# Duplicated feature columns by load, inverse deviations column by column, and x transposes between the tiles of the output projection, in a one-core adaLN transformer block

## The chip, the cores and the metric

The kernel runs on one core of a Trainium2 chip. The metric is the device time of one execution in microseconds (us). The core's engines are TensorE (PE in the rows; PEld its weight loads), VectorE (DVE), ScalarE (ACT), GpSimd (POOL) and SyncE (SP), which here issues nearly all DMAs.

## The reference

```python
mod = silu(c) @ w_mod                    # six vectors of 448: sa, ca, ga, sb, cb, gb
h = layernorm(x) * (1 + ca) + sa         # x: 2048 x 448, float32
q, k, v = split(h @ wqkv)                # 16 heads of 28
p = softmax(mask(q @ k.T * 28**-0.5))    # a key lies at most 255 positions back
x = x + ga * ((p @ v) @ wo)
h = layernorm(x) * (1 + cb) + sb
x = x + gb * (mish(h @ w1 + b1) @ w2)    # w1: 448 x 1792, w2: 1792 x 448
```

## The kernel before

The 2048 rows are worked through in four groups (g) of 512 rows, each four tiles of 128. Every product is done with split operands: a matrix is held as a high part (`hh`, `oh`, `wq3`, `Ph`) and the rest (`hl`, `ol`, `wql`, `Pl`), and a tile of a projection is eleven matmuls. The 448 features lie in four chunks of 128; the last chunk holds its 64 features twice, so that its high and low part share a matmul. That is why a normed row has 512 columns, the last 64 a copy of columns 384 to 447.

For a group, `gen_ln` (L226) takes the statistics of four row tiles on VectorE (`ln_stats`, L218), forms the inverse deviations `rs` on POOL (an add of epsilon, L234, and a power of -0.5, L235, each over four columns), norms the tiles on VectorE (L241), and copies the 64 columns on POOL (`dup`, L223). For the first norm that is done in place in `xin` (`gen_ln1`, L272), for group 0 of the second norm in `x1` (`gen_ln2`, L853); groups 1 to 3 of the second norm go by another way through DRAM (`gen_x1_ln2`, L1105). `gen_hT` (L287) then transposes the group's x on TensorE, one chunk of four 128x128 transposes per bank, two banks of the tag "mm" in turn; per chunk ScalarE makes `hh` (`hT_hi`, L256), and VectorE the scaled value in the bank (`hT_y`, L253) and `hl` (`hT_lo`, L259), after which the bank is free.

The attention is a hand-written loop over 192 units u, three per head and 48 per group. In a unit TensorE makes a block of scores (`B`, sB), the scores for a running maximum of a later head (`A`, sA; VectorE reduces them into mx, the line of junk), and the product with V of an earlier unit (`PV`); ScalarE makes P and Ph, and POOL one subtraction Pl = P - Ph (`SP`, L731). Between them the loop places other work, the fillers: `fill_main(g)` (L937) yields, for group g, the last three q/k tiles of g, then `gen_oT(g - 1)` (L614: transposes of the attention's output and their split), `gen_wo(g - 1)` (L637: the output projection by four tiles, whose sum with x, `xr`, and statistics `stw` VectorE takes), `gen_hT(g + 1)` and the first q/k and V tiles of g + 1. Each filler step names its cost in us, and each unit adds `RATE[g]` (L979) to a credit; steps are placed while the credit lasts. A second generator, `fill_side(g)` (L958), places small work once per unit. `pipe` (L29) delays the steps that follow a filler's matmuls by one step each.

The engines take their instructions in the order in which this program issues them, and SP its DMAs too. The tiles oT of the attention's output have the same names and buffers ("hh", "hl" of the pool `mid`) as the split x, so one waits for the readers of the other.

After the 192 units comes the second layer: 56 blocks n (14 per group) of a first product z, Mish on ScalarE and a second product acc.

## Time and profile before

| | |
|---|---|
| median of 3 runs | 708.94 us (708.24 to 710.24) |
| profiled execution | 708.93 us, of which the span 707.1 us |
| TensorE busy | 687.4 us |
| VectorE / ScalarE / POOL busy | 384.0 / 391.4 / 326.0 us |
| granted clock of TensorE | 1.00 of full speed |

The profile gives the busy time of each engine, in the whole span and in any window of it, the instructions in order of time with the idle time before each and what ended it, and groups of instructions by line, operation and shape with their mean duration. The attention of groups 0 to 3 takes the time to about 410 us, the second layer the rest.

### The profile page before, as it was taken

Reading aid. Unit: us, or ns where it says so; the run is one execution under the profiler, and the core shown is the slowest. Engines: PE = TensorE matmul, PEld = TensorE weight load, DVE = VectorE, ACT = ScalarE, POOL = GpSimd, SP = SyncE. Lnnn points to the kernel's source line nnn. Section 1 sums busy time; section 2 is a strip of 40 time slices with the busy share of each in tenths; the row PEclk is TensorE's granted clock in tenths of the full one; section 3 lists DMA queues with packets and bytes.
Section 4 is the critical chain, followed back from the end, with each engine's and each line's share of the span. In section 5 each row is a group of like instructions: output and inputs, shape, how many; then the busy total and the mean of one; then the engine's idle time right before and its main releaser. Section 6 shows DMA issues by size and latency. Waiting matters only on the chain.

```text
span 707.1 us, 12019 instructions
## 1 busy us (share of the span) xinstructions
PE 687.4 (97%) x4001; PEld 589.0 (83%) x4001; DVE 384.0 (54%) x1030; ACT 391.4 (55%) x740; POOL 326.0 (46%) x355
## 2 busy tenths in 40 slices
PE   8899999999999999999999999999999999999997
PEld 8777888888898788898887788887888888888886
DVE  5688667688664888555767765452314222422112
ACT  3638778767766867767877974344223322332221
POOL 6626779586766677666778957313010000000000
PEclk9999999999999999999999999999999999999999
DMA  7865664454672462762774155810340035001001
GB/s 211 256 224 182 216 198 160 136 163 151 191 214 71 152 194 91 189 208 78 230 217 141 54 195 159 238 25 1 104 110 10 1 105 116 4 1 52 1 1 52
DMA packets 75177, 90.16 MB, mean 127 GB/s; under 512 B 31534, under 2 KB 51740, under 8 KB 75116
## 3 DMA queue, kind: packets, MB, share of 16 engines
q1 hardware_dynamic: 74652, 89.39, 42.1%
q8 instruction: 32, 0.52, 0.3%
q14 instruction: 29, 0.24, 0.1%
q10 hardware_dynamic: 464, 0.00, 0.0%
HBM read 56.60 MB, written 32.51 MB: 126 GB/s over the span
## 4 chain that ended last, share of the span: by engine, by line
PE 77%; DVE 9%; ACT 4%; issue 3%; POOL 1%; DMA 0%; DVEq 0%; ACTq 0%; POOLq 0%
PE z L913 19%; PE pv L741 9%; PE qk L315 8%; PE acc L1098 6%; PE acc L1096 6%; PE acc L1097 6%; PE sA L679 5%; PE sB L709 4%; PE wo L315 4%; PE qk_v L315 4%; PE sB L720 3%; DVE junk L681 3%; PE et L755 2%; ACT P L723 1%; ACT Ph L724 1%
## 5 line engine op out<-in xcount | busy, mean ns | idle before, releaser
L731 POOL TENSOR_TENSOR Pl<-P,Ph 128x512 fp32r<-128x512 f32 (+2 forms) x192 | 234.3, 1228 | 83.2 <-ACT Ph L724 44.7
L681 DVE CUSTOM_DVE_ANT_0 junk<-sA,mask 128x384 f32<-128x384 f32 (+2 forms) x256 | 135.2, 528 | 96.5 <-PE sA L679 88.3
L723 ACT ACTIVATE P<-sB 128x512 f32<-128x512 f32 (+2 forms) x192 | 109.8, 572 | 63.3 <-PE sB L720 58.3
L921 DVE TENSOR_TENSOR al<-t,ah 128x512 fp32r<-128x512 f32 x56 | 39.2, 700 | 181.8 <-ACT ah L920 181.8
L919 ACT ACTIVATE t<-z,b1c 128x512 f32<-128x512 f32 x56 | 38.3, 684 | 138.6 <-PE z L913 138.6
L724 ACT ACTIVATE Ph<-sB 128x512 fp32r<-128x512 f32 (+2 forms) x192 | 109.2, 569 | 0.0
L679 PE MATMUL sA<-k,q 84*128 84x384 f32 (+2 forms) x256 | 100.9, 396 | 2.3 <-DVE mx L681 1.5
L913 PE MATMUL z<-hlf,w 128*128 128x512 f32 x224 | 88.5, 395 | 0.0
L913 PE MATMUL z<-hhf,w 128*128 128x512 f32 x224 | 88.5, 395 | 0.0
L1096 PE MATMUL acc<-w2h,ah 128*128 128x448 f32 x224 | 82.2, 367 | 1.2 <-ACT ah L920 1.2
L1098 PE MATMUL acc<-w2h,al 128*128 128x448 f32 x224 | 82.0, 366 | 0.0
L1097 PE MATMUL acc<-w2l,ah 128*128 128x448 f32 x224 | 81.5, 364 | 0.0
L741 PE MATMUL pv<-Pl,v 128*60 128x256 f32 (+2 forms) x352 | 74.0, 284 | 3.8 <-POOL Pl L731 2.8
L741 PE MATMUL pv<-Ph,v 128*60 128x256 f32 (+2 forms) x352 | 76.6, 291 | 0.6 <-ACT o L747 0.5
L709 PE MATMUL sB<-q,k 86*128 86x256 f32 (+1 forms) x352 | 74.0, 284 | 0.2
L913 PE MATMUL z<-hhf,w1l 128*128 128x512 f32 x168 | 66.2, 394 | 0.0
L709 PEld LDWEIGHTS sB<-q,k 86*128 86x128 f32 x352 | 61.5, 189 | 1.8 <-issue 0.6
L720 PE MATMUL sB<-fdmask,identr 128*128 128x128 bf16 (+1 forms) x320 | 60.1, 253 | 0.0
L741 PEld LDWEIGHTS pv<-Ph,v 128*60 128x60 f32 x352 | 45.5, 133 | 14.6 <-ACT o L747 2.4
L679 PEld LDWEIGHTS sA<-k,q 84*128 84x128 f32 x256 | 48.9, 192 | 8.7 <-DVE mx L681 6.0
L741 PEld LDWEIGHTS pv<-Pl,v 128*60 128x60 f32 x352 | 45.0, 131 | 13.2 <-POOL Pl L731 5.4
L913 PEld LDWEIGHTS z<-hlf,w 128*128 128x128 f32 x224 | 42.1, 188 | 10.1
(159 smaller groups left out, 1249.8 us busy)
## 6 DMA issues: line engine op xcount, KB each, us to landing
scr<-st SPq DMA_DIRECT2D x24, 512.0 KB
k<-scr SPq DMA_DIRECT2D x48, 252.0 KB
q<-scr SPq DMA_DIRECT2D x64, 168.0 KB
scr<-st SPq DMA_DIRECT2D x32, 256.0 KB
x<-x1d SPq DMA_DIRECT2D x10, 448.0 KB
xin<-in_A_x_dram SPq DMA_DIRECT2D x8, 448.0 KB
xr<-in_A_x_dram SPq DMA_DIRECT2D x16, 224.0 KB
x1d<-xr SPq DMA_DIRECT2D x16, 224.0 KB
```

The costliest lines, as they stand in the source:

```text
L315: PE.matmul(p, b, a, start=(n == 0), stop=(n == 10))
L679: PE.matmul(p[:, c0:384], q[0:84, t * 128:(t + 1) * 128], k[0:84, t * 128 + c0:t * 128 + 384], start=True, stop=True)
L681: DVE.tensor_tensor_reduce(out=junk[:, c0:384], in0=p[:, c0:384], in1=mask[:, c0:384], scale=1.0, scalar=-3.0e38, op0=ALU.add, op1=ALU.max ...
L709: PE.matmul(p[:, c:c + 128 * (t1 - t0)], k[:, jj * 128:(jj + 1) * 128], q[:, t0 * 128:t1 * 128], start=(n == 0), stop=False, skip_group_ch ...
L723: ACT.activation(P[:, c0:], p[:, c0:], AF.Exp, scale=SCALE)
L724: ACT.activation(Ph[u][:, c0:], p[:, c0:], AF.Exp, scale=SCALE)
L731: eng.tensor_tensor(Pl[u][:, a:b], Pt[u][:, a:b], Ph[u][:, a:b].bitcast(F32), op=ALU.subtract)
L741: PE.matmul(pv[0:60, t0 * 128:t1 * 128], V[j % NV][:, h, :], P[u][:, c:c + 128 * (t1 - t0)], start=(P is Ph and b == 0 and n == 0), stop=F ...
L913: PE.matmul(zb[n], ps[m][1], ps[m][0], start=(m == 0), stop=(m == 10))
L1096: PE.matmul(p, ah[n][:, ts], w2h[f], start=(f == 0), stop=False)
L1097: PE.matmul(p, ah[n][:, ts], w2l[f], start=False, stop=False)
L1098: PE.matmul(p, al[n][:, ts], w2h[f], start=False, stop=(f == NF - 1))
```

## The change

The loads of x for groups 1 to 3 (`x_half`), and of x1 for group 0 of the second norm (`x1_load`), get a second DMA that brings features 384 to 447 into columns 448 to 511; the norm there works in place on all 512 columns (`wide`), without `dup`. The inverse deviations are made column by column: VectorE adds epsilon to one column (`rs_add`), POOL raises it to -0.5 (`rs_pow`), one step later in `gen_ln`. For group 0 of the second norm they are made ahead, at the end of group 1's side work (`gen_rs2`). `gen_wo` takes a generator `beside` and places one step of it after each tile: for groups 1 and 2 that is `gen_hT(g + 1)`, one chunk after each tile of the output projection. The split output of the attention gets tiles of its own (tags "hho", "hlo" in the pool `att`), `ol` one buffer instead of two. A chunk is charged with 0.45 instead of 1.2 us (group 0's still 1.2), and the rate of groups 1 and 2 is 0.86 instead of 0.91.

```diff
--- before.py
+++ after.py
@@ -78,7 +78,7 @@
     qk, qk_s = pool("qk", side="right")
     ctx.enter_context(tc.manual_schedule())
 
-    cst.tile([128, 8], F32, name="lead")
+    rs2 = cst.tile([128, 8], F32, name="rs2")
     cT = cst.tile([112, 4], F32, name="cT")
     nc.scalar.dma_start(cT, c.rearrange("o (k p) -> p (o k)", p=112))
     ACT.add_instruction(mybir.InstLoadActFuncSet(
@@ -101,6 +101,8 @@
     def x_half(g, t):
         r = g * GT + t * 128
         dma(xin[g][:, t:t + 2, 0:D], xf[r:r + 256, :].rearrange("(t p) d -> p t d", p=128))
+        if g:
+            dma(xin[g][:, t:t + 2, D:512], xf[r:r + 256, 384:448].rearrange("(t p) d -> p t d", p=128))
 
     def x_load(g):
         x_tile(g)
@@ -223,27 +225,37 @@
     def dup(x):
         POOL.tensor_copy(x[:, D:512], x[:, 384:448])
 
-    def gen_ln(tiles, pl, xn_tiles, key, mv=None):
-        if mv is None:
-            mv = pl.tile([128, 4, 2], F32, name=f"mv{key}", tag="mv", bufs=2)
-            for t in range(4):
-                ln_stats(tiles[t], mv[:, t, :], pl, f"{key}{t}")
-                if t < 3:
-                    yield
-        rs = pl.tile([128, 4], F32, name=f"rs{key}", tag="rs", bufs=2)
-        POOL.tensor_scalar(rs, mv[:, :, 1], EPS, None, op0=ALU.add)
-        POOL.tensor_tensor(rs, rs, mhalf, op=ALU.pow)
-        yield
-        yield
+    def rs_add(rs, mv, t):
+        DVE.tensor_scalar(rs[:, t:t + 1], mv[:, t, 1:2], EPS, None, op0=ALU.add)
+
+    def rs_pow(rs, t):
+        POOL.tensor_tensor(rs[:, t:t + 1], rs[:, t:t + 1], mhalf[:, t:t + 1], op=ALU.pow)
+
+    def gen_ln(tiles, pl, xn_tiles, key, mv=None, rs=None, wide=False):
+        if rs is None:
+            rs = pl.tile([128, 4], F32, name=f"rs{key}", tag="rs", bufs=2)
+            stats = mv is None
+            if stats:
+                mv = pl.tile([128, 4, 2], F32, name=f"mv{key}", tag="mv", bufs=2)
+            for t in range(5):
+                if t < 4:
+                    if stats:
+                        ln_stats(tiles[t], mv[:, t, :], pl, f"{key}{t}")
+                    rs_add(rs, mv, t)
+                if t:
+                    rs_pow(rs, t - 1)
+                yield
         xs = xn_tiles()
         for t in range(4):
             xn = xs[t]
-            DVE.tensor_scalar(xn[:, 0:D], tiles[t], mv[:, t, 0:1], rs[:, t:t + 1],
+            n = 512 if wide else D
+            DVE.tensor_scalar(xn[:, 0:n], xn if wide else tiles[t], mv[:, t, 0:1], rs[:, t:t + 1],
                               op0=ALU.subtract, op1=ALU.mult)
-            if t:
+            if t and not wide:
                 dup(xs[t - 1])
             yield xs
-        dup(xs[3])
+        if not wide:
+            dup(xs[3])
 
     def tr_chunk(xs, ci, p):
         for t in range(4):
@@ -261,9 +273,9 @@
             hT_y(p, ci, si)
         DVE.tensor_tensor(hl[:, ci], p, hh[:, ci].bitcast(F32), op=ALU.subtract)
 
-    def new_T(key, pl):
-        return (pl.tile([128, 4, GT], F32R, name=f"hh{key}", tag="hh"),
-                pl.tile([128, 4, GT], F32R, name=f"hl{key}", tag="hl"))
+    def new_T(key, pl, own=""):
+        return (pl.tile([128, 4, GT], F32R, name=f"hh{key}", tag="hh" + own),
+                pl.tile([128, 4, GT], F32R, name=f"hl{key}", tag="hl" + own))
 
     V = [(vp if j < 6 else vq).tile([128, H, 60], F32R, name=f"v{j}") for j in range(NV)]
     done = set()
@@ -272,7 +284,7 @@
     def gen_ln1(g):
         def xn_tiles():
             return [xin[g][:, t] for t in range(4)]
-        for r in gen_ln([xin[g][:, t, 0:D] for t in range(4)], qk, xn_tiles, f"a{g}"):
+        for r in gen_ln([xin[g][:, t, 0:D] for t in range(4)], qk, xn_tiles, f"a{g}", wide=True):
             if r:
                 XS[g] = r
             yield "dve"
@@ -291,7 +303,7 @@
             p = bank("mm", 2, f"tr{g}{ci}")
             tr_chunk(XS[g], ci, p)
             pipe.add(2, lambda p=p, ci=ci: hT_hi(p, ci, hh, 0), lambda p=p, ci=ci: hT_lo(p, ci, hh, hl, 0))
-            yield 1.2
+            yield 1.2 if g == 1 else 0.45
         ht_done.add(g)
         if g + 1 < NG:
             loads = (lambda: x_load(g + 1),) if g > 1 else (lambda: (x_tile(g + 1), x_half(g + 1, 0)),
@@ -611,9 +623,9 @@
     on_full = set()
     XR = {g: {} for g in range(NG)}
 
-    def gen_oT(g, tag, bufs, oT_pool):
+    def gen_oT(g, tag, bufs, oT_pool, own=""):
         o = on[g]
-        oh, ol = OT[g] = new_T(f"o{g}", oT_pool)
+        oh, ol = OT[g] = new_T(f"o{g}", oT_pool, own)
 
         def oT_out(p, ci):
             DVE.tensor_tensor(ol[:, ci], p, oh[:, ci].bitcast(F32), op=ALU.subtract)
@@ -634,7 +646,7 @@
         XR[g][t] = xr_tile(f"xr{j}")[:, 0:D]
         dma(XR[g][t], xf[j * 128:(j + 1) * 128, :])
 
-    def gen_wo(g, tag, bufs):
+    def gen_wo(g, tag, bufs, beside=None):
         oh, ol = OT[g]
 
         def add(xr, p, t):
@@ -663,6 +675,10 @@
             w = yield from tile_mms(p[:, 0:D], [(b, a) for a, b in ps])
             pipe.add(1, lambda xr=xr, p=p, t=t: add(xr, p, t), lambda xr=xr, t=t: store(xr, t))
             yield w
+            if beside is not None:
+                yield next(beside)
+        if beside is not None:
+            yield from beside
 
 
     NS = NG * H
@@ -756,7 +772,7 @@
         et[pr] = p.rearrange("p (t a d) -> p t a d", t=4, a=2)
 
     def E2(pr):
-        olt[pr] = att.tile([128, 4, 2, 28], F32, name=f"ol{pr}", tag="ol", bufs=2)
+        olt[pr] = att.tile([128, 4, 2, 28], F32, name=f"ol{pr}", tag="ol", bufs=1)
         ACT.activation(olt[pr], et[pr][:, :, :, 32:60], AF.Copy)
 
     def E3(pr):
@@ -796,6 +812,8 @@
         for t in (0, 2):
             r = g * GT + t * 128
             dma(x1[g][:, t:t + 2, 0:D], x1d[r:r + 256, :].rearrange("(t p) d -> p t d", p=128))
+            if pl is FW["p1"] and g == 0:
+                dma(x1[g][:, t:t + 2, D:512], x1d[r:r + 256, 384:448].rearrange("(t p) d -> p t d", p=128))
 
     W1 = [(ci, c0) for c0 in range(0, F, D) for ci in range(4)]
     w1p = {}
@@ -818,6 +836,12 @@
     def piece_load(i):
         if i < len(SEQ):
             (w2_dma if SEQ[i][0] == "w2" else w1_load)(SEQ[i][1])
+
+    def gen_rs2():
+        for t in range(4):
+            rs_add(rs2, mv2[0], t)
+            rs_pow(rs2, t)
+            yield
 
     def gen_w1():
         for _ in range(3):
@@ -852,7 +876,8 @@
 
     def gen_ln2(g, pl, xn_tiles, tag, bufs):
         xs = None
-        for r in gen_ln([x1[g][:, t, 0:D] for t in range(4)], pl, xn_tiles, f"f{g}", mv=mv2[g]):
+        for r in gen_ln([x1[g][:, t, 0:D] for t in range(4)], pl, xn_tiles, f"f{g}", mv=mv2[g], rs=rs2,
+                        wide=True):
             xs = r or xs
             yield 0.6
         hh, hl = h2[g] = new_T(f"f{g}", (mid, FW.get("ff"))[g % 2])
@@ -944,10 +969,14 @@
                 w1_ready.add(g)
             while g - 1 not in on_full:
                 yield
-            yield from gen_oT(g - 1, "mm", 2, mid)
-            yield from gen_wo(g - 1, "mm", 2)
+            yield from gen_oT(g - 1, "mm", 2, att, "o")
+            if g + 1 < NG:
+                yield from gen_wo(g - 1, "mm", 2, gen_hT(g + 1))
+            else:
+                yield from gen_wo(g - 1, "mm", 2)
         if g + 1 < NG:
-            yield from gen_hT(g + 1)
+            if g == 0:
+                yield from gen_hT(1)
             yield from gen_qkv(g + 1, (0, 3, 4, 1) + VT)
         else:
             yield from finish()
@@ -961,6 +990,8 @@
             while g + 1 not in ht_done:
                 yield
             yield from lazy((gen_mod_wo, lambda: gen_mod_ln2(3), lambda: gen_mod_ln2(4))[g])
+            if g == 1:
+                yield from gen_rs2()
             if g == NG - 2:
                 yield from gen_out_load()
             return
@@ -976,7 +1007,7 @@
         if not (told.get(g) == "bank" and pipe.held() or told.get(g) in taken):
             told[g] = next(side[g], None)
 
-    RATE = {0: 0.56, 1: 0.91, 2: 0.91, 3: 0.65}
+    RATE = {0: 0.56, 1: 0.86, 2: 0.86, 3: 0.65}
     FRONT = {0: 0, 1: 2, 2: 2, 3: 2}
     ln1 = {g: gen_ln1(g) for g in range(1, NG)}
     fillers = {g: fill_main(g) for g in range(NG)}
```

What moves, at three places. The numbers in names tell unit, group or tile: Pl103 belongs to unit 103, xin3 and tr3 to group 3, wo1 to group 1.

VectorE, group 2, where group 3's x chunks follow the output projection of group 1. Before, between the split of chunk 0 and that of chunk 2:

```order
L254 TENSOR_SCALAR tr30_4035<-tr30_4035,cols_141 128x512
L262 TENSOR_TENSOR hl3_4034<-tr30_4035,hh3_4033 128x512
L681 ISA junk_479,mx42_4022<-sA42_3_4088,mask_154 128x384
L681 ISA mx42_4022 128x1
L254 TENSOR_SCALAR tr31_4061<-tr31_4061,cols_141 128x512
L262 TENSOR_TENSOR hl3_4034<-tr31_4061,hh3_4033 128x512
L681 ISA junk_479,mx42_4022<-sA43_0_4120,mask_154 128x384
L681 ISA mx42_4022 128x1
L254 TENSOR_SCALAR tr32_4096<-tr32_4096,cols_141 128x512
L262 TENSOR_TENSOR hl3_4034<-tr32_4096,hh3_4033 128x512
```

Now, from the split of chunk 1 to the sum of projection tile 2:

```order
L266 TENSOR_SCALAR tr31_3936<-tr31_3936,cols_141 128x512
L274 TENSOR_TENSOR hl3_3836<-tr31_3936,hh3_3835 128x512
L697 ISA junk_481,mx40_3859<-sA41_1_3987,mask_154 128x384
L697 ISA mx40_3859 128x1
L784 RECIPROCAL rc17_3990<-et17_3931 128x8
L785 TENSOR_TENSOR ol17_3964<-ol17_3964,et17_3931 128x224
L697 ISA junk_481,mx40_3859<-sA41_2_3998,mask_154 128x384
L697 ISA mx40_3859 128x1
L697 ISA junk_481,mx40_3859<-sA41_3_4017,mask_154 128x384
L697 ISA mx40_3859 128x1
L653 TENSOR_TENSOR xr6_3780<-xr6_3780,wo1_2_3966 128x448
L222 BN_STATS stw12_4032<-xr6_3780 128x6
```

Before, two chunks are one reduction of scores apart; now three reductions and a projection tile's sum and statistics stand between.

POOL, group 2, where the output of group 1 is completed (on1) and group 3's x is normed. Before:

```order
L234 TENSOR_SCALAR rsa3_3564<-mva3_3434 128x4
L235 TENSOR_TENSOR rsa3_3564<-rsa3_3564,mhalf_137 128x4
L731 TENSOR_TENSOR Pl102_3580<-P102_3548,Ph102_3549 128x512
L771 TENSOR_TENSOR on1_2299<-ol15_3559,rc15_3585 128x4x56
L773 COPY on1_2299<-on1_2299 128x4x64
L731 TENSOR_TENSOR Pl103_3618<-P103_3576,Ph103_3577 128x512
L731 TENSOR_TENSOR Pl104_3644<-P104_3614,Ph104_3615 128x512
L731 TENSOR_TENSOR Pl105_3677<-P105_3640,Ph105_3641 128x512
L731 TENSOR_TENSOR Pl106_3710<-P106_3673,Ph106_3674 128x512
L224 COPY xin3_2854<-xin3_2854 128x64
L731 TENSOR_TENSOR Pl107_3743<-P107_3706,Ph107_3707 128x512
L224 COPY xin3_2854<-xin3_2854 128x64
```

Now:

```order
L232 TENSOR_TENSOR rsa3_3448<-rsa3_3448,mhalf_137 128x1
L747 TENSOR_TENSOR Pl101_3569<-P101_3532,Ph101_3533 128x512
L232 TENSOR_TENSOR rsa3_3448<-rsa3_3448,mhalf_137 128x1
L747 TENSOR_TENSOR Pl102_3602<-P102_3565,Ph102_3566 128x512
L787 TENSOR_TENSOR on1_2309<-ol15_3576,rc15_3607 128x4x56
L789 COPY on1_2309<-on1_2309 128x4x64
L747 TENSOR_TENSOR Pl103_3641<-P103_3598,Ph103_3599 128x512
L232 TENSOR_TENSOR rsa3_3448<-rsa3_3448,mhalf_137 128x1
L747 TENSOR_TENSOR Pl104_3668<-P104_3637,Ph104_3638 128x512
L747 TENSOR_TENSOR Pl105_3701<-P105_3664,Ph105_3665 128x512
L747 TENSOR_TENSOR Pl106_3734<-P106_3697,Ph106_3698 128x512
L747 TENSOR_TENSOR Pl107_3766<-P107_3730,Ph107_3731 128x512
```

The add and the power of four columns, and the copies, are gone from the queue; powers of one column stand between the subtractions, the first of the four (not shown) behind Pl98.

POOL, end of group 3, where group 0's second norm is made. Before:

```order
L731 TENSOR_TENSOR Pl173_5734<-P173_5704,Ph173_5705 128x512
L234 TENSOR_SCALAR rsf0_5743<-mv2_0_475 128x4
L235 TENSOR_TENSOR rsf0_5743<-rsf0_5743,mhalf_137 128x4
L731 TENSOR_TENSOR Pl174_5759<-P174_5730,Ph174_5731 128x512
L771 TENSOR_TENSOR on3_5219<-ol27_5741,rc27_5764 128x4x56
L731 TENSOR_TENSOR Pl175_5785<-P175_5755,Ph175_5756 128x512
L731 TENSOR_TENSOR Pl176_5805<-P176_5781,Ph176_5782 128x512
L224 COPY x1_0_5429<-x1_0_5429 128x64
L731 TENSOR_TENSOR Pl177_5832<-P177_5801,Ph177_5802 128x512
L224 COPY x1_0_5429<-x1_0_5429 128x64
```

Now:

```order
L747 TENSOR_TENSOR Pl173_5756<-P173_5726,Ph173_5727 128x512
L747 TENSOR_TENSOR Pl174_5779<-P174_5752,Ph174_5753 128x512
L787 TENSOR_TENSOR on3_5239<-ol27_5763,rc27_5784 128x4x56
L747 TENSOR_TENSOR Pl175_5806<-P175_5775,Ph175_5776 128x512
L747 TENSOR_TENSOR Pl176_5826<-P176_5802,Ph176_5803 128x512
L747 TENSOR_TENSOR Pl177_5852<-P177_5822,Ph177_5823 128x512
```

Nothing of the second norm is left in POOL's queue here.

## Rows read from the trace of the kernel before

**Rows 1.** The page: busy us, share of the span and instructions of TensorE.

```profile
PE 687.4 (97%) x4001; PEld 589.0 (83%) x4001; DVE 384.0 (54%) x1030; ACT 391.4 (55%) x740; POOL 326.0 (46%) x355
```

**Rows 2.** Windows: length, then busy us and instructions; clock, DMA share, GB/s.

```profile
138.00:144.00 6.00, 5.31 (x41) 4.04 (x39) 5.33 (x18) 5.53 (x12) 5.35 (x7) 1.00 0.84 264
168.00:174.00 6.00, 5.21 (x45) 4.67 (x44) 5.55 (x16) 5.42 (x11) 4.59 (x4) 1.00 0.36 100
174.00:180.00 6.00, 5.91 (x42) 4.87 (x41) 5.79 (x18) 5.64 (x11) 4.28 (x5) 1.00 0.25 86
```

**Rows 3.** In order of time: start, us, engine, line; idle us before, what ended it.

```profile
138.51 0.23 POOL L234 TENSOR_SCALAR rsa<-mva 128x4 f32<-128x4 f32 x1 [1.23 <-DVE mva L221]
138.82 1.05 POOL L235 TENSOR_TENSOR rsa<-rsa,mhalf 128x4 f32<-128x4 f32 x1
...
141.18 0.44 PE L741 MATMUL pv<-Pl,v 128*60 128x128 f32 x2 [0.28 <-POOL Pl L731]
...
143.41 0.44 PE L741 MATMUL pv<-Pl,v 128*60 128x256 f32 x2 [0.40 <-POOL Pl L731]
...
172.34 0.63 PE L250 MATMUL tr<-ident,xin 128*128 128x128 f32 x4 [0.79 <-DVE hl L262]
...
274.18 0.30 PE L250 MATMUL tr<-ident,xin 128*128 128x128 f32 x1 [0.79 <-DVE hl L262]
```

**Rows 4.** Windows at the end of group 3, columns as in rows 2.

```profile
384.00:390.00 6.00, 4.83 (x33) 3.43 (x32) 5.40 (x15) 4.39 (x10) 5.92 (x7) 1.00 0.27 89
390.00:396.00 6.00, 5.64 (x45) 4.95 (x45) 4.90 (x16) 5.47 (x12) 6.00 (x8) 1.00 0.02 4
```

**Rows 5.** Groups on VectorE by shape: count, busy us, mean ns of one, idle before.

```profile
L681 DVE CUSTOM_DVE_ANT_0 junk<-sA,mask 128x384 f32<-128x384 f32 x224 | 123.9, 553 | 82.1 <-PE sA L679 77.5
...
L254 DVE TENSOR_SCALAR tr<-tr,cols 128x512 f32<-128x512 f32 x14 | 11.4, 814 | 0.7 <-ACT hh L257 0.7
...
L262 DVE TENSOR_TENSOR hl<-tr,hh 128x512 fp32r<-128x512 f32 x16 | 11.1, 691 | 0.8 <-ACT tr L457 0.4
...
L220 DVE BATCH_NORM_STATS2 stw<-xr 128x6 f32<-128x448 f32 x16 | 10.0, 627 | 0.6
...
L641 DVE TENSOR_TENSOR xr<-xr,wo 128x448 f32<-128x448 f32 x16 | 9.8, 614 | 1.2 <-PE wo L315 1.0
...
L414 DVE TENSOR_SCALAR sT<-sT 112x4 f32<-112x4 f32 x1 | 0.1, 136 | 0.0
```

**Rows 6.** Groups on POOL by shape, columns as in rows 5.

```profile
L731 POOL TENSOR_TENSOR Pl<-P,Ph 128x512 fp32r<-128x512 f32 x155 | 201.4, 1304 | 76.2 <-ACT Ph L724 39.3 <-PE pv L741 10.6 <-PE sA L679 9.0
...
L235 POOL TENSOR_TENSOR rsa<-rsa,mhalf 128x4 f32<-128x4 f32 x3 | 3.1, 1042 | 0.2
...
L403 POOL TENSOR_TENSOR rs<-rs,mhalf 128x2 f32<-128x2 f32 x2 | 1.6, 781 | 0.2
...
L224 POOL COPY x<-x 128x64 f32<-128x64 f32 x4 | 1.5, 364 | 0.0
```

**Rows 7.** Windows, columns as in rows 2.

```profile
132.00:138.00 6.00, 6.00 (x45) 5.24 (x44) 4.03 (x13) 4.27 (x9) 3.17 (x3) 1.00 0.60 184
210.00:216.00 6.00, 6.00 (x42) 5.49 (x42) 3.11 (x13) 3.60 (x8) 3.00 (x4) 1.00 0.52 188
```

**Rows 8.** The norm's line L241: shortest, median and longest in ns.

```profile
L241 DVE TENSOR_SCALAR xin<-xin,mva,rsa x12: 497/854/1504, 41.9 to 256.3; 128x448 f32<-128x448 f32 x12
```

**Rows 9.** Windows, columns as in rows 2.

```profile
24.00:30.00 6.00, 6.00 (x30) 5.39 (x29) 3.16 (x4) 4.46 (x10) 5.06 (x4) 1.00 0.98 305
42.00:48.00 6.00, 5.63 (x28) 4.30 (x26) 5.81 (x20) 0.60 (x1) 0.95 (x4) 1.00 0.59 207
450.00:456.00 6.00, 6.00 (x29) 5.24 (x28) 2.56 (x5) 2.07 (x4) 1.15 (x1) 1.00 0.97 215
```

**Rows 10.** In order of time, columns as in rows 3: SP and TensorE in the start.

```profile
20.89 1.03 SPq L59 DMA_DIRECT2D xin<-in_A_x_dram  x2
...
34.75 0.30 PE L679 MATMUL sA<-k,q 84*128 84x128 f32 x1 [0.43 <-DMA k<-scr]
```

## What the change was predicted to do

> **What bounds the kernel now.** I read the page's busy times first: TensorE is busy for 97% of the span [rows 1]. So nothing can be won but the stretches where it waits, and I took these from the busy times in windows of 6 us. In the attention part the windows in which TensorE falls short recur at two places of each group: 5.31 of 6 us at 138 us, and 5.21 and 5.91 at 168 to 180 us [rows 2]. The list of instructions in time says why. At 138 us the POOL queue gets the group's inverse deviations, an add of 0.23 and a power of 1.05 us, between two Pl subtractions; the PV matmuls then wait 0.28 and 0.40 us for Pl [rows 3]. At 172 us the third x transpose waits 0.79 us for VectorE's hl of the first: the transposes have two banks, four chunks come in a row, and VectorE is at 5.55 and 5.79 of 6 us there [rows 2, 3]. The same wait of 0.79 us stands at 274.18 us [rows 3], so group 2 repeats group 1; 48 units lie between, hence 101.84 / 48 = 2.12 us per unit. A third place is the end of group 3: TensorE has 4.83 and 5.64 of 6 us, and POOL 5.92 and 6.00, so POOL is the bound there [rows 4]. All other idle time of TensorE (the start, group 0, the last chain of group 3) is touched only where I say so. A matmul's end is modelled, so small waits hide in "busy": the idle times shown are lower bounds.
>
> **The change, part by part.** The profiled execution took 708.93 us, its span 707.1; the median of the runs shown is 708.94, so a sum made against the profiled one stands for the median. The runs reach from 708.24 to 710.24, so about 0.3% (2.1 us) is what a measurement can tell from no change.
>
> *Transposes between the output projection's tiles (groups 1 and 2).* No instruction is added. Per chunk VectorE has hT_y 0.81 and hT_lo 0.69 us [rows 5], four chunks 6.0 us; now they come within some 12 us, in which VectorE is busy 11.34 us [rows 2]. By the order they come to lie one per tile. A tile and its chunk give VectorE 0.61 + 0.63 + 0.81 + 0.69 = 2.74 us [rows 5] and a small aggregation; they hold the fillers for about 3.1 units (by the kernel's own costs 2.24 us of projection and 0.45 for a chunk, at 0.86 a unit), which is 6.5 us. The reductions of the scores add 4/3 x 0.55 per unit [rows 5], 2.3 us. That is 5.0 of 6.5 us, and with the small operations near 85%: busy, no longer full. The bank is not asked for again until a whole tile has passed, so the 0.79 us goes. Own tiles for the oT splits are needed so that the chunks need not wait for the projection to have read its operands. Saved at least the 0.88 us idle of the two windows [rows 2], less what a fuller VectorE gives back later: between 0 and 1.2 us a group; I take 0.8, near the idle that the rows show.
>
> *Inverse deviations by column.* Per group the POOL queue loses one add and one power of four columns (1.05 + 0.23 us [rows 3]) and four copies of 64 columns at 0.36 [rows 6]. It gains four powers of one column. No row shows one; four columns take 1.04 and two 0.78 us [rows 6], so 0.13 a column and 0.65 for one; it lies between 0.52 (no column) and 0.78. In sum POOL has about the same work (2.6 for 2.7 us), but spread over six units, where it has room: it is busy 3.17 of 6 us in the window before [rows 7]. Between the two Pl that now wait, one power of 0.65 stands in place of 1.28 us, and behind them no copy waits for VectorE's xin. The output's own multiply and copy stay in that place. Of the idle 0.69 us [rows 2] I take 0.6 with what is hidden; the ends are 0 (VectorE, 5.33 of 6 us there, holds the stretch anyhow) and 1.0. VectorE gains four adds per group; the nearest row is a scalar add of four columns, 0.14 us [rows 5], together 0.55 us where it is busy 4.03 of 6 us [rows 7]: hidden. The norm on 512 columns adds 64 to 448: from the 0.50 us that the shortest took [rows 8], at most 0.07 us each.
>
> *Group 0 of the second norm.* Its four powers and adds move to the end of group 1, where POOL is busy 3.00 and VectorE 3.11 of 6 us [rows 7]: nothing. At its old place POOL loses an add and a power, 1.28 us by group 1's [rows 3], and four copies of 0.36 [rows 6], 2.7 us in all, in 12 us in which it hardly rests [rows 4]. TensorE's idle time there is 1.17 + 0.36 = 1.53 us; the next bound is close, VectorE with 5.40 and 4.90, ScalarE with 5.47 in the second window [rows 4]. I take 1.2 us, ends 0.3 and 2.0.
>
> *Loads.* Eight further DMAs. The two for group 1 stand in SP's queue behind the weights and ahead of the first stores to scr. SP has room: it issues the two xin in 1.03 us at 20.89 us, and TensorE, not SP, is late for the first scores only by a landing, 0.43 us [rows 9, 10]. But the transfers share full queues: 98% busy at 305 GB/s [rows 9]. 131 KB more takes 0.43 us at that rate, and 0.61 at the 215 GB/s of the window in which pieces of 128 bytes move [rows 9]. The first scores wait for just this chain, so I charge 0.6 us; ends 0 and 0.9. The other six fall where DMA has room, with loads two slots ahead of their use: nothing. VectorE is near full in group 0's norm (5.81 of 6 us [rows 9]) and gets four adds and the wider norm, 0.8 us, while one wait for POOL goes: I charge 0.2, ends 0 and 0.7.
>
> *The rest.* The rates 0.86 and 0.45 spread the same fillers over the same 48 units; the last V tiles stand at the same units as before. The later norms of the second layer's groups end one block of 5 us later, two blocks before they are used: nothing. One buffer for ol instead of two: its next writer comes six units later: nothing.
>
> The sum: 708.9 - 2 x (0.8 + 0.6) - 1.2 + 0.6 + 0.2 = 705.7 us.
>
> **The rivals.**
>
> *POOL's queue waits for the adds (slower).* A power stands in POOL's line ahead of a Pl subtraction, and can start only when VectorE has made its add; at 138.51 us the add of before waited 1.23 us idle for VectorE's statistics [rows 3]. POOL has 2.12 - 1.30 [rows 6] = 0.82 us room per unit, and a power takes 0.65, so a wait of w beyond 0.17 us delays Pl, and so PV. There are twelve powers in groups 1 and 2 (four of them for the second norm). It turns into a loss against 708.9 when 12 x (w - 0.17) is over the 3.2 us won, w over 0.44; at w = 0.65 it costs 5.8 us and gives 711.5. For it: VectorE is behind near the clump. Against: by the order each power is issued a step, hence a unit or more, after its add. Chance 0.08.
>
> *VectorE stays the bound (no change).* With 94% before and some 85% by my sum in the mixed stretch, a few waits for the reductions can eat the whole of 2 x 0.8: 707.3 us. The norm of xin shows how: of twelve the shortest took 0.50, the median 0.85 and the longest 1.50 us [rows 8]; it stretches where POOL is busy. The Trainium skill, in "SBUF — State Buffer", section "Who interferes with whom", says that VectorE's scalar operations between SBUF tiles in their two-port mode and GpSimd take a shared port pair in turn, each for a whole instruction; the trace agrees, and by that rule an added scalar add can wait as well. Four adds, each waiting the longest 1.0 us, would make 4.5 us in 12.7 us with some 4 us to spare [rows 7, 8], so at most 0.5 us a group, 1.0 in all, which by itself leaves 706.7. Chance 0.18 for 707.3 or so.
>
> *More than the sum.* If all idle time that the windows show goes, with what hides in "busy" (the upper ends: 2 x (1.2 + 1.0) + 2.0, against 0.2 for the loads), it is 702.7 us. Chance 0.16.
>
> *The place changes, the time doesn't.* That the transposes do stand between the tiles, and the copies are gone, the order shows. But the time won may be asked back at the end of each group, where scores wait for the new group's rows by way of scr: 708.5 us. Chance 0.08.
>
> **The numbers.** The forecast, 705.7, has 0.50. Faster by over 0.3% (below 706.8) are the forecast's case, the larger gain and a little of the VectorE case: 0.50 + 0.16 + 0.02 = 0.68. Within 0.3%: 0.16 + 0.08 = 0.24. Slower: 0.08. The range takes in the larger gain, and above the cases of no change up to some loss: 702.3 to 709.4.
>
> **What would show it.** Right: no wait of an x transpose for hl in groups 1 and 2, window sums of TensorE above 5.8 at 168 to 180 us, no copy of xin on POOL, 0.6 to 0.7 us for a power of one column, TensorE over 10.9 of the 12 us at the end of group 3, and the first scores half a microsecond later. Wrong: PV waits for Pl that ends behind a power, adds of a microsecond on VectorE, scores waiting for mx between projection tiles, or a group that still takes 101.8 us.

## The result, and the profile after

The changed kernel takes 711.67 us in the median (18 runs, 709.54 to 715.10) against 708.94 of the kernel before, a ratio of 1.004 with a 95% interval of 1.003 to 1.0051. It is slower by 2.7 us. The forecast was 705.7 us, with a range of 702.3 to 709.4: wrong in sign and outside the range. The profiled execution of the changed kernel took 710.33 us, its span 708.5, so it is one of the shorter of the 18.

The page of the changed kernel, busy us of each engine, answers to [rows 1]:

```profile
PE 685.8 (97%) x4001; PEld 590.4 (83%) x4001; DVE 386.2 (55%) x1058; ACT 392.4 (55%) x740; POOL 329.6 (47%) x353
```

VectorE has 28 instructions more (the adds by column) and 2.2 us more work. TensorE has the same 4001 instructions and less busy time, in a longer span: it waits more. The windows of the changed kernel, columns as in [rows 2], say where:

```profile
138.00:144.00 6.00, 5.57 (x48) 4.95 (x47) 5.10 (x18) 5.91 (x12) 5.58 (x7) 1.00 0.83 266
150.00:156.00 6.00, 3.47 (x27) 2.95 (x26) 4.57 (x12) 3.10 (x7) 4.33 (x4) 1.00 0.75 245
168.00:174.00 6.00, 6.00 (x45) 5.44 (x44) 5.38 (x15) 4.46 (x9) 4.01 (x4) 1.00 0.24 64
174.00:180.00 6.00, 6.00 (x43) 5.28 (x42) 4.83 (x13) 4.14 (x8) 3.66 (x4) 1.00 0.75 224
384.00:390.00 6.00, 4.53 (x31) 3.12 (x30) 5.65 (x17) 4.80 (x11) 4.27 (x4) 0.95 0.45 155
390.00:396.00 6.00, 6.00 (x41) 5.52 (x42) 4.90 (x14) 4.12 (x8) 5.11 (x5) 0.77 0.02 4
```

The places that the prediction looked at have become better: 5.57 for 5.31 us at 138 us, and TensorE full from 168 to 180 us, where it had 5.21 and 5.91 [rows 2]. Two things are new. From 150 to 156 us TensorE works only 3.47 of 6 us. And from 384 to 396 us TensorE's granted clock, the last column but two, is 0.95 and 0.77, where it was 1.00 [rows 4]. The instructions of the changed kernel in order of time at these places, columns as in [rows 3]:

```profile
146.13 0.44 PE L695 MATMUL sA<-k,q 84*128 84x384 f32 x1 [0.83 <-DVE mx L697]
...
152.28 1.27 POOL L747 TENSOR_TENSOR Pl<-P,Ph 128x512 fp32r<-128x512 f32 x1
...
153.83 1.26 POOL L747 TENSOR_TENSOR Pl<-P,Ph 128x512 fp32r<-128x512 f32 x1 [0.28 <-POOL Pl L747]
...
153.93 1.44 DVE L252 TENSOR_SCALAR xin<-xin,mva,rsa 128x512 f32<-128x512 f32 x1
...
155.43 0.33 PE L262 MATMUL tr<-ident,xin 128*128 128x128 f32 x1 [2.53 <-DVE xin L252]
...
257.61 0.33 PE L262 MATMUL tr<-ident,xin 128*128 128x128 f32 x1 [2.54 <-DVE xin L252]
...
385.40 1.40 POOL L747 TENSOR_TENSOR Pl<-P,Ph 128x512 fp32r<-128x512 f32 x1 [0.20 <-POOL Pl L747]
...
385.70 1.59 DVE L202 TENSOR_TENSOR w<-w1p,w 64x448 fp32r<-64x448 f32 x1
...
387.94 0.45 PE L695 MATMUL sA<-k,q 84*128 84x384 f32 x1 [1.35 <-DVE mx L697]
...
388.46 0.40 PE L757 MATMUL pv<-Pl,v 128*60 128x128 f32 x2
...
390.55 0.63 PE L757 MATMUL pv<-Pl,v 128*60 128x256 f32 x2
```

At 155.43 and 257.61 us the last of the four transposes of the first chunk waits 2.5 us for the norm of the fourth tile of x. That norm began at 153.93, a tenth of a microsecond behind a Pl of POOL, and lasted 1.44 us: to 155.37, 0.28 behind the end of that Pl at 155.09. At 385.70 VectorE's subtract of a weight piece meets a Pl in the same way and lasts 1.59 us; the scores behind it wait 1.35 us, and after that standstill TensorE's rows are longer: a pair of PV matmuls that takes 0.40 us at full clock takes 0.63. The groups of the changed kernel on VectorE and POOL, columns as in [rows 5]:

```profile
L252 DVE TENSOR_SCALAR xin<-xin,mva,rsa 128x512 f32<-128x512 f32 x12 | 10.0, 830 | 0.0
...
L229 DVE TENSOR_SCALAR rsa<-mva 128x1 f32<-128x1 f32 x12 | 1.9, 154 | 0.4
```

```profile
L232 POOL TENSOR_TENSOR rsa<-rsa,mhalf 128x1 f32<-128x1 f32 x12 | 6.5, 543 | 7.4 <-DVE rsa L229 7.4
```

An add by column takes 0.15 us, where 0.14 was forecast, and a power 0.54 us, where 0.65 was. The 7.4 us in which POOL waited for adds all lie between 31 and 41 us, in group 0 and before the first Pl.

### The profile page after: what moved, and what is told of

Its sections match the earlier page's. It is cut to its first block, busy times and chain, and to the rows that moved or that the text cites. A ratio compares the mean times of both kernels' runs of the same rounds, so it can differ in the third digit from the quotient of the medians.

```text
span 708.5 us, 12027 instructions
## 1 busy us (share of the span) xinstructions
PE 685.8 (97%) x4001; PEld 590.4 (83%) x4001; DVE 386.2 (55%) x1058; ACT 392.4 (55%) x740; POOL 329.6 (47%) x353
## 4 chain that ended last, share of the span: by engine, by line
PE 84%; DVE 6%; DMA 3%; ACT 3%; issue 2%; SPq 1%; POOL 0%; DVEq 0%; POOLq 0%; ACTq 0%
PE z L938 19%; PE pv L757 10%; PE qk L327 8%; PE acc L1129 6%; PE acc L1127 6%; PE acc L1128 6%; PE sA L695 6%; PE sB L725 5%; PE wo L327 5%; PE qk_v L327 4%; PE sB L736 4%; PE et L771 2%; DMA scr<-st 2%; DVE junk L697 1%; PE warm L440 1%
```

## The experiments

Ratios are to the kernel before, run on the same chip beside each, with their 95% intervals; medians in us. "Clock" is the mean granted clock of each run. The kernel before had medians of 708.73 to 709.05 us beside these kernels, so medians of two rows can be compared to within about 0.3 us, and by their ratios otherwise.

| kernel | median us | ratio | clock, run by run |
|---|---|---|---|
| before, again | 708.63 | 1.0001 [0.9992, 1.001] | 0.997 to 1.000 |
| the change | 711.67 | 1.004 [1.003, 1.0051] | 0.990 to 0.999 |
| e1 transposes a tile later | 711.23 | 1.004 [1.0025, 1.0056] | 0.992 to 1.000 |
| e2 all but the move | 709.62 | 1.0013 [1.0004, 1.0021] | 0.997 to 1.000 |
| e3 the move alone | 706.62 | 0.9969 [0.9958, 0.998] | 0.999 to 1.000 |
| e5 change + idle power | 714.58 | 1.0077 [1.0064, 1.0091] | 0.990 to 0.997 |
| e6 change, second norm later | 713.45 | 1.0062 [1.0046, 1.0077] | 0.993 to 0.997 |
| e7 e3 + early norms | 704.02 | 0.9936 [0.9924, 0.9948] | 0.998 to 1.000 |
| e8 e3 + wide norms | 712.21 | 1.0046 [1.003, 1.0061] | 0.992 to 0.997 |
| e9 change + early norms | 705.49 | 0.9958 [0.9945, 0.9971] | 0.994 to 1.000 |
| e10 e9 + second norm later | 705.11 | 0.9947 [0.9934, 0.9959] | 0.999 to 1.000 |
| e11 e7 + wide norms | 705.67 | 0.9958 [0.9946, 0.997] | 0.997 to 1.000 |
| e12 e8 + filled wait | 709.85 | 1.0016 [1.0005, 1.0027] | 0.998 to 1.000 |
| e13 e8 + copies | 707.70 | 0.9984 [0.9972, 0.9997] | 0.995 to 1.000 |
| e14 change + copies | 708.15 | 0.9988 [0.9978, 0.9997] | 0.995 to 1.000 |
| e15 e7 + by-column | 703.52 | 0.9914 [0.99, 0.9929] | 0.999 to 1.000 |

### First series: which part loses?

**before, again** (no edit).

> The kernel before against itself, for TensorE's granted clock run by run. Theory A (the 2.5 us waits of the first x transpose are the loss; they and the granted clock that falls after such a standstill make the longer time): ratio 1.000 within 0.002, granted clock 0.999 to 1.000 in nearly every run. Rival C (the granted clock wanders on this chip whatever the kernel, and the changed kernel's clocks of 0.990 to 0.999 say nothing): clocks between 0.990 and 0.999 here too, with times that fall as the clock rises.

Ratio 1.0001, all eleven clocks at 0.997 or more, and in the profile none below 1.00 before the last 6 us of the span. So rival C is out: clocks under 0.997 come only with the changed kernel and some of the kernels below.

**e1, transposes a tile later.**

```diff
-            if beside is not None:
+            if beside is not None and t:
                 yield next(beside)
```

> The changed kernel with its x transposes beginning behind the second output projection tile and not the first. Theory A (the first transpose stands in TensorE's order ahead of the moment at which VectorE has normed the fourth tile of x): the waits of 2.53 and 2.54 us at 155 and 258 us fall under 0.6 us, the time goes from 711.7 to 706.5 to 708.5, and the mean clock rises towards 1.0. Rival B (the by-column powers and the wide norm made the deviations late, so that whoever uses them waits): the wait moves with the transpose and stays over 1 us, time 710 to 712. Rival C (clock only): waits gone, clock still 0.990 to 0.997, time 709.5 to 711.

The wait for the norm is gone and another takes its place, which none of the three theories had: two chunks are now left for the end, and the q/k tile behind them waits 2.21 us for VectorE's hl. The time is the same within the intervals, so theory A's 706.5 to 708.5 is missed. It lies in rival B's range, but the wait is for the split of a chunk and not for a norm.

```profile
175.30 0.47 PE L327 MATMUL qk<-hh,wq 128*128 128x512 f32 x1 [2.21 <-DVE hl L274]
```

**e2, all but the move.**

```diff
-            if g + 1 < NG:
-                yield from gen_wo(g - 1, "mm", 2, gen_hT(g + 1))
...
+            yield from gen_wo(g - 1, "mm", 2)
         if g + 1 < NG:
-            if g == 0:
-                yield from gen_hT(1)
+            yield from gen_hT(g + 1)
```

(and the charge 1.2 and the rate 0.91 again.)

> The changed kernel with the x transposes behind the last output projection tile again, at the old rates; wide loads, by-column deviations and the second norm as changed. Theory A: no wait of the transposes for a norm, and the other parts of the change keep what they give: 707 to 709 (the kernel before less 0 to 2). Rival B (the loss is in the by-column deviations, the wide norm or the added loads): 710 to 712, about as the changed kernel.

709.62 lies between the two expectations, 0.9 above the kernel before. The parts that were to win 2.4 us win nothing; the wait of 1.35 us for mx and a low clock (0.88 and 0.84 from 384 to 396 us) are in its profile too.

**e3, the move alone**, put into the kernel before.

```diff
+            if beside is not None:
+                yield next(beside)
+        if beside is not None:
+            yield from beside
...
-            yield from gen_wo(g - 1, "mm", 2)
+            if g + 1 < NG:
+                yield from gen_wo(g - 1, "mm", 2, gen_hT(g + 1))
```

(with the own tiles, the one buffer of ol and the new charge and rate.)

> The kernel before with the move of the x transposes alone (own buffers, the new rates); norms of 448 columns, copies and whole-group deviations on GpSimd as before. Theory A: the first transpose waits at 155 and 258 us for the norm of tile 3 and its copy on GpSimd, as long as in the changed kernel or longer (2.5 to 4 us each), time 711 to 714. Rival B: no wait over 1 us there, time 706 to 708.

Theory A's number is missed by far: 706.62 us, 2.1 less than before. The transposes do overtake the norm, but wait only 1.60 us, and the move wins in spite of that. The time is in rival B's range; the wait fits neither expectation. The trace of e3, in order of time:

```profile
152.73 0.51 DVE L241 TENSOR_SCALAR xin<-xin,mva,rsa 128x448 f32<-128x448 f32 x1
...
153.30 0.33 PE L250 MATMUL tr<-ident,xin 128*128 128x128 f32 x1 [1.60 <-DVE xin L241]
153.30 0.24 POOL L224 COPY xin<-xin 128x64 f32<-128x64 f32 x1 [0.78 <-DVE xin L241]
...
153.50 1.28 POOL L735 TENSOR_TENSOR Pl<-P,Ph 128x512 fp32r<-128x512 f32 x1
...
253.98 0.33 PE L250 MATMUL tr<-ident,xin 128*128 128x128 f32 x1 [1.60 <-DVE xin L241]
```

POOL stands idle for 0.78 us, since its next instruction is the copy of the fourth tile's 64 columns, which needs the norm. So no Pl runs beside that norm, and it takes 0.51 us. Without the copy POOL would go on to Pl.

The copies alone did not shelter that norm. In the kernel before, which has them too, the fourth norm of the same group began 0.03 us behind a Pl:

```profile
154.51 1.28 POOL L731 TENSOR_TENSOR Pl<-P,Ph 128x512 fp32r<-128x512 f32 x1 [0.90 <-POOL xin L224]
...
154.54 1.49 DVE L241 TENSOR_SCALAR xin<-xin,mva,rsa 128x448 f32<-128x448 f32 x1
```

It took 1.49 us there, and nobody waited for it, since the transposes came only at 167.8 us. Its copy stood behind the Pl. The move makes `gen_hT` run what is left of the norms at once, so that in e3 the fourth norm's copy stands directly behind that of the third tile and ahead of the next Pl.

### Second series: VectorE behind Pl

Theory D came from these traces: a norm of VectorE, or a subtract of two SBUF tiles, that begins inside a Pl lasts until that Pl is over. Not all of VectorE's work is held so: in the changed kernel the statistics of a tile, begun at 152.72 us inside the Pl of 152.28, took their usual 0.63 us.

**e5, an idle power** ahead of the second norm of group 0.

```diff
+        else:
+            POOL.tensor_scalar(rsd, mv[:, :, 1], EPS, None, op0=ALU.add)
+            POOL.tensor_tensor(rsd, rsd, mhalf, op=ALU.pow)
         xs = xn_tiles()
```

> The changed kernel with the addition and the power over four columns put back on GpSimd ahead of the second norm of group 0, their result used by nobody: work added, nothing else moved. Theory D (VectorE's subtract of a weight piece at 385.7 us meets GpSimd's Pl, runs until Pl ends, 1.59 us and not 0.62, the scores wait 1.35 us for mx, and TensorE's granted clock falls behind that standstill; a power on GpSimd in that place lets VectorE through): the subtract takes 0.6 to 0.8 us, the wait of 1.35 us falls under 0.5, the clock is 1.00 from 387 to 393 us, and the time falls from 711.7 to 708 to 709.8. Rival E (GpSimd's time is what counts and the clock falls for a reason of its own): 1.3 us more on GpSimd, time 711.5 to 713, clock low at the same place.

At its place it did what D says. The kernel before had the same pair, and in its rows the subtract begins ahead of the power:

```profile
384.02 0.62 DVE L200 TENSOR_TENSOR w<-w1p,w 64x448 fp32r<-64x448 f32 x1
...
384.26 1.28 POOL L235 TENSOR_TENSOR rsf<-rsf,mhalf 128x4 f32<-128x4 f32 x1
```

In e5 the subtract begins inside the power and still takes 0.62 us, and the scores wait 0.40 us; in order of time:

```profile
388.39 1.10 POOL L251 TENSOR_TENSOR rsd<-rsd,mhalf 128x4 f32<-128x4 f32 x1
...
388.62 0.62 DVE L203 TENSOR_TENSOR w<-w1p,w 64x448 fp32r<-64x448 f32 x1
...
389.89 0.44 PE L699 MATMUL sA<-k,q 84*128 84x384 f32 x1 [0.40 <-DVE mx L701]
```

But the time rose to 714.58. The windows of e5 show what took the gain:

```profile
156.00:162.00 6.00, 6.00 (x32) 5.29 (x30) 3.66 (x11) 2.35 (x6) 2.58 (x2) 0.72 0.38 107
...
258.00:264.00 6.00, 5.38 (x27) 4.71 (x28) 3.48 (x8) 2.43 (x5) 1.57 (x2) 0.72 0.01 3
384.00:390.00 6.00, 5.61 (x44) 4.67 (x42) 5.31 (x17) 5.82 (x12) 5.46 (x6) 1.00 0.64 174
390.00:396.00 6.00, 5.10 (x35) 3.76 (x36) 5.26 (x16) 4.46 (x10) 6.00 (x6) 1.00 0.04 11
```

The clock is 1.00 at 384 to 396 us, as expected, but 0.72 behind each of the two waits of 2.5 us, where the profiled execution of the changed kernel had kept 1.00. So its time says nothing of the place that was edited. The expectation of 708 to 709.8 is missed.

**e6, the second norm two steps later.**

```diff
+        else:
+            yield
+            yield
         xs = xn_tiles()
```

> The changed kernel with the second norm of group 0 begun two steps later, as it was before, so that VectorE's subtract of the weight piece stands ahead of the first norm again; no work added. Theory D: the subtract begins before Pl does, 0.6 to 0.8 us, no wait of the scores over 0.5 us at 388, clock 1.00 from 387 to 393 us, time 708 to 709.8. Rival F (the wide norms themselves hold VectorE, wherever they stand): the wait moves to the next scores, over 1 us, the clock falls there, time 711 to 712.

The same: the subtract takes 0.62 us, no score waits over 0.5 us there, the clock is 1.00 from 384 to 396 us, and the time is 713.45, with a clock of 0.73 and 0.52 behind the two waits of 2.5 us. Why these two kernels lost more there than the changed kernel itself stays open.

**e7, e3 with the norms of x one step earlier.**

```diff
         yield
-        yield
+        if key[0] != "a":
+            yield
```

> The kernel before with the move of the x transposes alone, and with the norms of x one step earlier. Theory A (the first transpose stands in TensorE's order ahead of VectorE's norm of the fourth tile: a wait of 1.60 us in each of two groups): both waits fall under 0.5 us, time from 706.6 to 703.5 to 705.6. Rival G (VectorE is full there, and what it does earlier for the norm it does later for others): waits of the scores for mx or of the transposes take their place, 706 to 707.2.

704.02 us, as theory A expects. What the earlier norms would give without the move, no run shows. The fourth norm is over before the transposes begin, and these run without a wait:

```profile
149.25 0.50 DVE L242 TENSOR_SCALAR xin<-xin,mva,rsa 128x448 f32<-128x448 f32 x1
...
151.99 0.60 PE L251 MATMUL tr<-ident,xin 128*128 128x128 f32 x4
```

**e8, e3 with the wide loads and norms of x** (deviations and second norms as before).

```diff
+        if g:
+            dma(xin[g][:, t:t + 2, D:512], xf[r:r + 256, 384:448]...)
...
-            if t:
+            if t and not wide:
                 dup(xs[t - 1])
```

> The kernel before with the move of the x transposes and the loads and norms on 512 columns for x; deviations over four columns on GpSimd, second norms as before. If the wide norm is what made the wait of the first transpose 2.53 us and not 1.60 (it starts inside a Pl and runs to its end): that wait is 2.3 to 2.6 us here and the time 707.8 to 709.5. If the by-column deviations did it (other places on GpSimd, and so of Pl): the wait stays 1.4 to 1.7 us and the time is 705.5 to 707.

This is the losing part: 712.21, that is 5.6 us above e3, and more than the whole change takes. The wait is the one expected of the wide norm; the time is 2.7 us above the range that went with it. The trace of e8, in order of time, and its windows:

```profile
153.17 1.26 POOL L739 TENSOR_TENSOR Pl<-P,Ph 128x512 fp32r<-128x512 f32 x1 [0.28 <-POOL Pl L739]
...
153.28 1.44 DVE L244 TENSOR_SCALAR xin<-xin,mva,rsa 128x512 f32<-128x512 f32 x1
...
154.77 0.47 PE L254 MATMUL tr<-ident,xin 128*128 128x128 f32 x1 [2.53 <-DVE xin L244]
...
155.47 0.63 PE L749 MATMUL pv<-Pl,v 128*60 128x128 f32 x2
...
161.19 0.40 PE L749 MATMUL pv<-Pl,v 128*60 128x128 f32 x2
...
257.84 0.33 PE L254 MATMUL tr<-ident,xin 128*128 128x128 f32 x1 [2.54 <-DVE xin L244]
```

```profile
150.00:156.00 6.00, 3.47 (x23) 2.93 (x22) 4.57 (x12) 3.44 (x6) 3.71 (x4) 0.87 0.71 233
156.00:162.00 6.00, 6.00 (x36) 5.30 (x35) 3.78 (x11) 2.61 (x6) 2.57 (x2) 0.85 0.24 64
...
258.00:264.00 6.00, 6.00 (x43) 5.42 (x43) 4.07 (x12) 3.66 (x7) 2.57 (x2) 1.00 0.22 62
```

The wait is 2.53 us to the hundredth, as in the changed kernel, with the norm again a tenth behind a Pl. In this execution the clock fell behind the first wait and not behind the second: the same form of matmul takes 0.63 us at 155.47 and 0.40 at 161.19.

### Third series: the remedy, and the clock

**e9, the change with early norms.**

```diff
-                yield
+                if t < 4 or key[0] != "a":
+                    yield
```

> The changed kernel, all parts kept, with the norms of x one step earlier. Theory A+D (the transposes overtake the fourth norm; the wide norm makes that wait 2.53 us since no copy on GpSimd holds Pl back any more; TensorE's clock falls behind it in some executions): no wait of a transpose over 0.5 us at 155 and 258 us, clock 1.00 from 150 to 162 and 252 to 264 us; the wait of 1.35 us and the low clock at 388 to 393 us stay; time 705.5 to 708. Rival G (VectorE is full there, the wait comes up elsewhere): 709.5 to 711.5.

705.49 us, 6.2 less than the change and at the lower edge of what was expected; the waits at 155 and 258 us are gone, and the wait of 1.34 us for mx and, in the profile, the low clock at 384 us (0.79) stay. The profiled execution is the longest of the six, 708.09 us; its clock is low at 36 to 42 us too (0.73), in the start.

**e10, the same with the second norm two steps later** (the edits of e9 and e6).

> The same, and the second norm of group 0 two steps later as before. Theory A+D: both waits gone, clock 1.00 from the first score to the last, 704 to 706.5, within 1.5 us of the kernel with the early norms and none of the other parts (704.0). Rival H (the by-column deviations, the wide loads or the second norm lose time for a reason of their own): over 707.5.

705.11, as theory A+D expects, and no clock below 1.00 before the last 6 us of the span. Against e9 the median is 0.4 lower, which the overlapping intervals don't tell from nothing: in the trace the place of the 1.34 us now has a wait of 1.09 us, of a transpose for the second norm. The scores' wait for mx at 147 us, 1.03 us in each of two groups, is still there.

**e11, e7 with the wide loads and norms.**

> The kernel before with the move of the x transposes, the norms one step earlier, and the wide loads and norms of x. Theory A+D: with the fourth norm out of the transposes' way the wide norm costs nothing: 703 to 705, clock 1.00. If the wide loads or norms cost by themselves: 706 or more.

705.67 lies between the two expectations, 1.7 above e7. No wait of the transposes is left, and the mx wait at 147 us of e10 isn't there either. Whether the wide loads and norms cost something by themselves is not settled: the intervals of e7 and e11 overlap.

**e12, e8 with the wait filled.**

```diff
+            if t == 3:
+                for _ in range(fill):
+                    PE.transpose(p[:, 384:512], xs[2][:, 0:128], ident)
```

> The move of the x transposes with the wide loads and norms (712.2 us measured, the waits of 2.53 us in it, clock low behind them), with 18 transposes that nobody reads put between the third and the fourth tile's transpose in groups 2 and 3, so that TensorE works through the wait and nothing comes sooner. If the clock that falls behind the standstill is a cost of its own: clock 1.00 in 150 to 162 and 252 to 264 us, mean clock 0.998 or more, time 708 to 709.7. If the wait alone is the cost: 711.5 to 713. If TensorE's own rows explain the clock (dense work lowers it): clock lower than in the run without the filler.

The fourth transpose comes no sooner, but TensorE works meanwhile. In order of time, and the windows:

```profile
153.09 2.13 PE L256 MATMUL tr<-ident,xin 128*128 128x128 f32 x18
...
155.79 0.33 PE L257 MATMUL tr<-ident,xin 128*128 128x128 f32 x1 [0.57 <-DVE xin L244]
...
257.47 0.33 PE L257 MATMUL tr<-ident,xin 128*128 128x128 f32 x1 [0.58 <-DVE xin L244]
```

```profile
150.00:156.00 6.00, 5.43 (x45) 4.95 (x44) 5.01 (x13) 3.26 (x7) 4.36 (x4) 1.00 0.91 298
156.00:162.00 6.00, 6.00 (x44) 5.42 (x43) 4.11 (x12) 3.70 (x7) 2.57 (x2) 1.00 0.25 64
```

Work that nobody uses makes the kernel 2.4 us faster: 709.85 for 712.21, with every clock at 0.998 or more, against 0.997 and less. The median is 0.15 above the upper end of the expected range. So the lower clock cost e8 about 2.4 us (2.1 by the ratios). The traces agree: from the wait in group 1 to that in group 2, e8 takes 103.07 us (154.77 to 257.84), with one fall of the clock, and e12 101.68 (155.79 to 257.47), with none, that is 1.4 us a fall. The 3.2 us that e12 still lies above e3 are the held norms and what the wide loads and norms cost by themselves.

### Fourth series: the copies

**e13, e8 with the copies put back.**

```diff
-            if t and not wide:
+            if t and (not wide or key[0] == "a"):
                 dup(xs[t - 1])
```

> The move of the x transposes with the wide loads and norms (712.2 us, waits of 2.53 us), and GpSimd's copies of 64 columns put back behind the wide norms, writing what stands there already. Theory D2 (a copy that waits for its norm holds the next Pl back, so that the fourth norm runs alone; without it Pl starts first and the norm lasts until Pl ends): the fourth norm takes 0.5 to 0.6 us and not 1.44, the first transposes wait 1.5 to 1.7 us, the clock stays 1.00 from 150 to 162 us, time 706 to 708. Rival (512 columns and four more loads are the cost): waits of 2.5 us and 711.5 to 713 again, or more by the copies' 0.4 us each.

707.70 us: the copies write what is there already, and save 4.5 us. The trace of e13 reads like that of e3:

```profile
152.72 0.55 DVE L244 TENSOR_SCALAR xin<-xin,mva,rsa 128x512 f32<-128x512 f32 x1
...
153.32 0.33 PE L254 MATMUL tr<-ident,xin 128*128 128x128 f32 x1 [1.64 <-DVE xin L244]
153.33 0.24 POOL L226 COPY xin<-xin 128x64 f32<-128x64 f32 x1 [0.81 <-DVE xin L244]
...
153.52 1.28 POOL L739 TENSOR_TENSOR Pl<-P,Ph 128x512 fp32r<-128x512 f32 x1
...
254.07 0.33 PE L254 MATMUL tr<-ident,xin 128*128 128x128 f32 x1 [1.64 <-DVE xin L244]
```

From wait to wait e13 takes 100.75 us and e3 100.68, the same. The 101.68 of e12, with the held norm and the full clock, are 0.93 us more: that is the price of the held norm.

**e14, the whole change with the copies put back** (the same edit).

> The whole change, with the copies of 64 columns of x put back on GpSimd and nothing else. Theory D2: the waits of 2.53 us fall to 1.4 to 1.8, no low clock behind them; the wait of 1.35 us at 388 us and the low clock there stay: 708 to 710. Rival: 711.5 to 714.

708.15 us, as expected: 3.5 less than the change, and the ratio 0.9988 [0.9978, 0.9997] is no longer a loss. The waits of the transposes are 1.64 us. The wait of 1.34 us for mx at the end of group 3 is there, yet in this execution no clock fell behind it.

**e15, e7 with the deviations of x by column** (copies, loads and second norms as before).

```diff
+        if key[0] == "a":
...
+                    rs_add(rs, mv, t)
+                if t:
+                    rs_pow(rs, t - 1)
```

> The kernel with the move and the norms one step earlier (704.0 us), and the deviations of x by column; copies, second norms and loads as before. If the by-column powers shift Pl onto an early norm (the whole change shows the scores waiting 0.8 to 1.0 us for mx at 146 us in each of two groups, and the wide loads alone do not): that wait is here, 705 to 706.5. If they relieve GpSimd as predicted: no such wait, 702.5 to 704.

703.52 us, the second of the two expectations, and the fastest of all: 5.5 us below the kernel before. It is 0.5 us below e7 by the medians and 1.6 by the ratios, whose intervals just overlap. No score waits for mx over 0.45 us in groups 1 and 2. So the by-column powers do no harm by themselves. In the changed kernel the scores wait 0.83 and 0.85 us for mx at 146 and 248 us, and in e14, with the copies back, 0.85 and 0.83; e2, without the move, has no such wait. What it takes besides the powers and the move stays open.

## Why the prediction was wrong

*The transposes between the tiles: the right mechanism, the size by luck.* Forecast were 2 x 0.8 = 1.6 us; e3, the move alone, wins 2.1 (0.2 to 0.42% by its interval, 1.4 to 3.0 us). The sign to look for came: in the changed kernel no x transpose waits for hl any more, and 168 to 180 us is full. What the term missed is that the first chunk now stands in TensorE's order ahead of VectorE's norm of the fourth tile: a wait of 1.60 us a group in e3, put at nothing. With the norms earlier (e7) the wait is gone and the gain is 4.8 us. So the forecast's 1.6 is near e3's 2.1 because a larger gain and an unforeseen wait nearly cancel.

*The copies and the wide norm: this step failed.* The prediction put the four copies of 64 columns down as work that POOL loses, and the wider norm as "at most 0.07 us each". Both are true of the work, and both miss the order: once the move had put the fourth copy ahead of the next Pl (e3), it waited for its norm, POOL stood idle meanwhile, and that idle time was what the norm ran in. Without it the fourth norm took 1.44 us for 0.51 (e8 against e3), 0.93 us a group on the path to the transposes; the waits of 1.60 became 2.53 us, and TensorE's clock fell behind them. Of the 5.6 us between e3 and e8, 2 x 0.93 = 1.9 are the longer waits and 2.4 the clock (e12). The remaining 1.3 us are close to what e13 lies above e3 (1.1 us), with the same waits and the copies in both. Since the two take the same from wait to wait, this lies elsewhere: the added loads, or the spread between runs, which the overlapping intervals of e3 and e13 don't tell apart.

*The row was there.* Among the norms of the kernel before the shortest took 0.50 and the longest 1.50 us [rows 8], and the rival "VectorE stays the bound" quoted them, for the price of added adds. It should have asked which norms begin inside a Pl, before and after POOL's queue is emptied, and who would now wait for them. That is the Trainium skill's rule too, in "SBUF — State Buffer", section "Who interferes with whom": when VectorE runs in a two-port mode, whichever of it and GpSimd issues first holds the shared port pair for its whole instruction. The trace agrees: 1.44 us for a norm that begins 0.10 us after a Pl, 0.51 to 0.55 for one alone.

*By column: the right direction, the size not settled.* Forecast were 2 x 0.6 us for powers and copies together. Alone, with the copies kept, it is 0.5 us in all by the medians of e15 and e7, and not surely more than nothing. The adds cost 0.15 us each, inside a Pl too (at 129.67 us in one that began at 129.54), and behind the first Pl no power waited for one. So the rival on POOL's queue is out, and the longer adds that the rival on VectorE allowed for did not come.

*The second norm: a wrong step.* 1.2 us were to come from 2.7 us less work on POOL. In its place Pl moved up and VectorE's subtract met it: 1.59 for 0.62 us, a wait of 1.35 us for mx, and a low clock in the profiles of the change, e1, e2 and e9. e5 and e6 undid the meeting, but their times are overlaid by the other clock losses, and e10 lies only 0.4 us below e9. TensorE has 10.53 of 12 us there, some of them at the low clock, and not the 10.9 that were to show the step right. What the second norm alone is worth stays open.

*Clock: left out.* The prediction had no term for it, since the clock was 1.00 in the whole trace of before. It took every wait at its own length.

*Loads.* 0.8 us were charged for added loads and group 0's norm. The first scores begin at 34.5 us and not half a microsecond later than the 34.75 of before [rows 10]; what the added loads and wider norms cost is at most about what e13 lies above e3 and e11 above e7, 1.1 and 1.7 us, and the intervals overlap in both pairs.

*The sum.* The terms that hold (the move 2.1, by column 0.5) would give about 706.3 us, near the forecast, and by luck, since the move's 2.1 has the unforeseen wait in it. With the copies back the whole change takes 708.15 (e14); without them 711.67, so this step cost 3.5 us. The 1.8 us from 706.3 to 708.15 are not taken apart: the second norm's wait, the scores' waits for mx at 146 and 248 us and the added loads lie in them. From the first chunk's wait in group 1 to that in group 2 the changed kernel takes 102.18 us (155.43 to 257.61), where the forecast named 101.8 as the sign of no gain. The same change with the norms a step earlier (e9) gives 705.49.

## What to carry to other kernels

Before an operation is taken off a queue, ask what it holds back: here POOL's queue, while a copy waited for VectorE, left VectorE undisturbed, and four copies of no use (e13) were worth more than their time. Where instructions are moved to an earlier place, write down for each what it waits for on another engine, where that stands in that engine's own order, and how long it takes there: the fourth norm's 1.49 us could be read before the change. And a standstill of TensorE like the ones here (1.35 and 2.53 us) is to be priced above its length: by what the rows behind it take when the clock falls (1.4 us a fall between e8 and e12).

## What the runs showed of the hardware

TensorE's granted clock can fall to its lower level (1.2 for 2.4 GHz) behind a single wait in a stretch that is otherwise full, and it does so in some executions only. Behind 2.53 us it fell in e5 and e6 at both places, in e8 at the first and not at the second, and in the profiled execution of the change at neither. Behind the wait of 1.31 to 1.35 us for mx at the end of group 3 it fell in the profiles of the change, e1, e2 and e9, and not in e14's. Behind the two waits of 2.21 us in e1 and of 1.60 us in e3 it didn't fall in the profile, and all seven runs of e3 had 0.999 or more; e13, with two waits of 1.64 us, kept it in its profile, but had runs down to 0.995. What decides it is not shown. The changed kernel's 18 runs spread over 5.6 us where before's spread over 2.6, and six of its seven longest, 712.35 to 715.10 us, have clocks of 0.990 to 0.994.

A norm or a subtract of two SBUF tiles on VectorE that begins inside POOL's 128x512 subtraction ends 0.3 to 0.5 us after it (the norm at 155.37 for 155.09 us, the subtract at 387.29 for 386.80, both in the change). A tile's statistics (0.63 us at 152.72) and an add of one column (0.15 us at 129.67) take their usual time there, and so does the subtract inside POOL's power of four columns (0.62 us at 388.62 in e5).
